# Crossbar-DMA transposes and full-array scores in a fused recurrent-attention and feed-forward kernel

## The chip, the cores and the metric

The kernel runs on one core of one Trainium2 chip. The time is device microseconds of one execution of the whole program. Before the change it is 191.06 us, the median of 3 runs (190.56, 191.06, 191.49). Beside the runs there is one profiled execution, from which all views of the profile come.

The core has a matrix engine (TensorE, PE in the profile; its weight loads are PEld), a vector engine (DVE), an activation engine (ACT), GpSimd (POOL) and SyncE (SP). SP computes nothing here: it issues every DMA of this kernel, in program order, on one queue.

## What is computed

Gated linear attention with a decay per key channel, then a feed-forward layer with a squared relu:

```python
# q, k, v, alpha: (4, 8, 768, 48), alpha in 0.8 to 1.0; w_in: (384, 2048); w_out: (2048, 384)
for t in range(S):
    state = alpha[:, :, t, :, None] * state + einsum('bhd,bhe->bhde', k[:, :, t], v[:, :, t])
    y[:, :, t] = einsum('bhd,bhde->bhe', q[:, :, t], state)
x = y.transpose(0, 2, 1, 3).reshape(3072, 384)
h = maximum(x @ w_in, 0)
out = (h * h) @ w_out          # (3072, 384) float32
```

## The kernel before

**Tiling.** The 4 x 768 tokens are 24 chunks of 128 tokens (6 for each batch entry). A chunk of the attention part makes one token tile of x, and the feed-forward part (called MoE in the code) works on tiles of 128 tokens, in groups of 4, 1, 1, and then 2.

**A chunk of attention** (`add_chunk(s)`, from line 358). Four loads of 192 KB bring alpha, q, k and v. ACT takes the logarithm of alpha (L379); a matmul with a triangular matrix sums it along the tokens (p0); ACT makes A, the exponential of the sum, and its inverse (L408, L412). DVE makes qA = q times A (L431) and kI = k times the inverse (L434), in bf16, with each head padded from 48 to 64 columns, so that two heads fill 128 columns. POOL casts v to bf16 (vb, L388). Then:

- p1q and p1k (L438 to L447): four PE transposes of 128x128 each, of qA and of kI, into one PSUM bank pT.
- cp, cpk (L449 to L458): copies from PSUM to the SBUF tile qkT, whose first four blocks are q transposed and whose last four are k transposed. Chunks 0 to 3 (`EARLY`) make two copies of 128x512, the others one of 128x1024 on DVE.
- p2 (L460 to L467): the scores sc, eight matmuls with 64 rows each: head `2p` lies in partitions 0 to 63 and head `2p+1` in 64 to 127 of block p.
- sm (L472): two masked products on DVE from PSUM to SBUF.
- ps, stm, sb (L482 to L498): the state, updated from kI and vb, decayed on DVE, cast on ACT for the next chunk.
- p3a, p3b: the output of the chunk, from q transposed and the state, and from sm and vb. xn (ACT), p4 (three PE transposes) and xT (DVE) put it into xT_big as the feed-forward's input.

kI, qA and the logarithm have 4 buffers each (`NBUF`), loads 6 (`LB`), qkT 4, r 8, the output tiles 6.

**The feed-forward part.** add_moe1: matmuls with w_in, a relu on ACT to r (L577), its square on DVE to gT (L585). add_moe2: 16 matmuls with w_out for a tile, a copy from PSUM (L617, or L615 on DVE), and an output DMA (L622).

**The order.** Nothing is scheduled at run time: each engine runs its instructions in the order in which they are written. That order comes from `Plan.run`, a list scheduler in the kernel's own Python, which works with planned durations. Each `Op` has an engine (or several to choose from), a duration, what it depends on, a priority, the PSUM bank it takes, and a latency `lat` after its end. The scheduler picks what can start earliest, then the lower priority number; attention has -10, MoE matmuls 0 or 0.1. `ready` adds a slack for PE to every dependency on another engine: 0.05, and 0.25 after the first 25 planned us. "DMA" is the planner's engine for loads, in their given order; "OUT" stands for output DMAs, which also take time from "DMA". `late` puts an operation further back in the final order than it was planned. At the end all operations are sorted by their planned start and written out, so the loads and outputs of SP's queue stand in that order too.

**The gate.** A chunk's p0 may be planned only when its number is at most `LEAD` (3.5) plus the tiles of MoE work already planned; each tile counts 2.56 for w_in and 2.56 for w_out.

Of the kernel before, what the change touches and what calls it, by code (L numbers as in the profile page):

```python
# [9 lines left out]
BF16 = mybir.dt.bfloat16  # L10
# [23 lines left out]
LAT = {"PE": 0.13, "ACT": 0.14, "DVE": 0.13, "POOL": 0.25}  # L34
PE_SLACK = 0.05
PE_CALM = 25.0


class Op:
# [15 lines left out]
def after(op, x=0.0):  # L55
    return (op, x)


class Plan:
# [13 lines left out]
    def ready(self, op):  # L73
        t = op.at
        slack = PE_SLACK if "PE" in op.durs else 0.0
        if slack and self.free.get("PE", 0.0) > PE_CALM:
            slack = 0.25
        for d, x in op.deps:
            if d.done is None:
                return None  # L80
            if x is None:
                t = max(t, d.done + (slack if d.eng != "PE" else 0.0))
            else:
                t = max(t, d.start + d.dur + x)
        if op.takes is not None:
            best = None
            for sl in op.takes:
                f = sl.free_at()
                if f is not None and (best is None or f < best):
                    best, op.slot = f, sl  # L90
            if best is None:
                return None
            t = max(t, best)
        return t

    def run(self, gate):
        free = self.free
        while any(self.pending.values()):
            best = None
            for eng, ops in self.pending.items():  # L100
                t0 = free.get(eng, 0.0)
                pick = None
                fifo = eng in ("DMA",)
                for op in (ops[:1] if fifo else ops):
                    if not gate(op):
                        continue
                    r = self.ready(op)
                    if r is None:
                        continue
                    if len(op.durs) > 1:  # L110
                        ends = {e: max(r, free.get(e, 0.0)) + x + LAT[e] for e, x in op.durs.items()}
                        if ends[eng] > min(ends.values()):
                            continue
                    key = (max(r, t0), op.prio)
                    if pick is None or key < pick[0]:
                        pick = (key, op)
                if pick is not None and (best is None or pick[0][0] < best[0]):
                    best = (pick[0][0], eng, pick[1])
            assert best is not None, "nothing can run"
            t, eng, op = best  # L120
            for e in op.durs:
                self.pending[e].remove(op)
            op.eng, op.dur = eng, op.durs[eng]
            op.start = t + getattr(op, "late", 0.0)
            free[eng] = t + op.dur
            if op.lat is None:
                op.lat = LAT.get(eng, 0.2)
            if eng == "OUT":
                free["DMA"] = max(free.get("DMA", 0.0), t) + op.dur
            op.done = t + op.dur + op.lat  # L130
            if op.takes is not None:
                self.ready(op)
                op.slot.release.append(op.gives if op.gives is not None else op)
            self.order.append(op)
            self.on_pick(op)
        self.order.sort(key=lambda o: o.start)
# [3 lines left out]
def kernel(  # L140
# [10 lines left out]
    nc = tc.nc  # L151
    B, H, S, D = q.shape
    HD = H * D
    P = 128
    DP = 64
    NP = H // 2
# [14 lines left out]
    big = ctx.enter_context(tc.tile_pool(name="big", bufs=1))  # L171
    LB = 6
    loads = ctx.enter_context(tc.tile_pool(name="loads", bufs=LB))
    work = ctx.enter_context(tc.tile_pool(name="work", bufs=4))
# [17 lines left out]
        out=utri_f, in_=utri_f, compare_op=ALU.is_ge, fill=0.0,  # L192
# [10 lines left out]
    for c in range(JN):  # L203
        blk = slice(JP * c, JP * c + JP)
        nc.gpsimd.affine_select(
            out=tri4[blk, 0:JW], in_=tri4[blk, 0:JW], compare_op=ALU.is_ge, fill=0.0,
# [17 lines left out]
    nc.gpsimd.memset(qA_s[:, :, :, D:], 0.0)  # L224
    kI_s = big.tile([P, NBUF, H, DP], BF16)
    nc.gpsimd.memset(kI_s[:, :, :, D:], 0.0)
    ae_s = big.tile([P, NBUF, NP, 2], FP32)
    nc.vector.memset(ae_s, 0.0)
    xT_big = big.tile([P, KT, n_tok], BF16)
# [4 lines left out]
    def pin(ins):  # L234
        tc.keep_in_program_order(ins)

    def mm(*a, **kw):
        pin(nc.tensor.matmul(*a, **kw))  # L238

    def tr(*a):  # L240
        pin(nc.tensor.transpose(*a))  # L241

    plan = Plan()
    sl_sc = Slots(1)
# [3 lines left out]
    GLA_BANKS = sl_bank[0:2]  # L248
# [12 lines left out]
    def add(eng, dur, emit, *deps, **kw):  # L261
        return plan.add(Op(eng, dur, emit, deps, **kw))
# [41 lines left out]
    C = [dict() for _ in range(NT)]  # L304
    state = {}
    SRC = dict(srcs)
    EARLY = 4

    JLD = 1.18
    J = {}  # L310
# [47 lines left out]
    def add_chunk(s):  # L358
        d = C[s]
        b, c = divmod(s, NCH)  # L360
        i = s % NBUF
        L, qA, kI, ae = L_s[:, i], qA_s[:, i], kI_s[:, i], ae_s[:, i]
        old = C[s - NBUF].get("end") if s >= NBUF else None
        g = dict(prio=-10.0 + s * 0.01)
        last = c == NCH - 1

        def cast(op, out_t, in_t):
            if op.eng == "ACT":
                pin(nc.scalar.copy(out_t, in_t))  # L369
            elif op.eng == "DVE":  # L370
                pin(nc.vector.tensor_copy(out_t, in_t))  # L371
            else:
                pin(nc.gpsimd.tensor_copy(out_t, in_t))
# [8 lines left out]
        else:  # L382
            ln = [add("ACT", 0.41, e_ln, d["ld_at"], old, prio=-15.0 if s < EARLY else -5.0)]
            d["use_at"] = ln[0]
# [50 lines left out]
        mq = d["use_qt"] = add("DVE", 0.47, e_qA, a_, d["ld_qt"], old, **g)  # L435
        mk = d["use_kt"] = add("DVE", 0.47, e_kI, ai, d["ld_kt"], old, **g)
# [6 lines left out]
        def e_p1k():  # L443
            for p in range(NP):
                tr(d["pT"][:, NP + p, :], kI[:, 2 * p:2 * p + 2, :], ident_bf)
        p1q = plan.add(Op("PE", 0.22, e_p1q, [mq], takes=GLA_BANKS, **g))
        p1k = plan.add(Op("PE", 0.22, e_p1k, [mk, after(p1q)], lat=0.15, **g))  # L447

        def e_cp(lo, hi):  # L449
            if lo == 0:  # L450
                d["qkT"] = work.tile([P, 2 * NP, P], BF16, name="qkT")
            cast(cpk if lo else cp, d["qkT"][:, lo:hi, :], d["pT"][:, lo:hi, :])
        if s < EARLY:
            cp = add({"ACT": 0.49, "DVE": 0.34}, 0, lambda: e_cp(0, NP), p1q, **g)
            cpk = add({"DVE": 0.34, "ACT": 0.49}, 0, lambda: e_cp(NP, 2 * NP), p1k, after(cp, -9.0), **g)
        else:
            cp = cpk = add("DVE", 0.61, lambda: e_cp(0, 2 * NP), p1k, **g)
        p1q.gives = cpk  # L458

        def e_p2():  # L460
            sc = d["sc"] = ps_sc.tile([P, 2, NP, P], FP32, name="sc")
            t = d["qkT"]
            for p in range(NP):
                for hh in range(2):
                    sl = slice(64 * hh, 64 * hh + 64)
                    mm(sc[:, hh, p, :], lhsT=t[sl, NP + p, :], rhs=t[sl, p, :], start=True, stop=True)
        p2 = plan.add(Op("PE", 0.42, e_p2, [cp, cpk], takes=[sl_sc], lat=0.10, **g))  # L467

        def e_sm(hh):
            if hh == 0:  # L470
# [60 lines left out]
        def e_xT():  # L531
            cast(xT, xT_big[:, :, s * P:(s + 1) * P], d["px"])
        xT = add({"ACT": 0.36, "DVE": 0.27} if s < EARLY else "DVE", 0.27, e_xT, p4, prio=-9.0)
        d["x"] = d["end"] = xT
# [95 lines left out]
    for d in DMA_ORDER + list(range(6, NT)):  # L630
        if d in ("i", "o"):
            load_w(d)
        elif d == "at":
            add_joint_alpha()
        elif isinstance(d, tuple):
            add_load(*d)
            if d == JLAST:
                for s in range(JN):
                    add_chunk(s)
        else:  # L640
            for nm, _ in srcs:
                add_load(d, nm)
            add_chunk(d)
# [23 lines left out]
                b2 = add_moe2(g, tt, b2, {}, range(NQ), M2_LAST if g >= NG - 2 else M2_BANKS)  # L667
        sq[(g, "free")] = b2

    LEAD = 3.5  # L670

    def gate(op):
        s = getattr(op, "gla", None)
        if s is not None:
            return s <= LEAD + (prog["m1"] + prog["m2"]) / 5.12
        return True
# [58 lines left out]
```

## Time and profile before

| what | value |
|---|---|
| runs | 191.06 us median of 3, 190.56 to 191.49 |
| span of the profiled execution | 189.9 us |
| copies to qkT of 128x1024, DVE, x20 | 690 ns each |
| copies to qkT of 128x512, DVE x3, ACT x5 | 422 and 588 ns each |
| qA, kI on DVE, x24 each | 572 and 576 ns each |
| masked scores sm on DVE, x48 | 683 ns each |
| square gT on DVE, x96 | 428 ns each |
| relu r on ACT, x96 | 604 ns each |
| first matmul (p0) of chunks 5, 11, 12, 13, 16, 22, 23 | 43.9, 76.5, 83.4, 90.3, 111.7, 154.0, 161.2 us |
| last load issued; last chunk's xT | 122.0; 169.7 us |

Times inside the program count from the start of the span. In a row of a timeline the first number is the start and the second how long it lasted; for rows with xN, N instructions are merged. A matmul's end is modelled, so neighbouring rows overlap and it is the starts that tell the pace. In a row of the windows the busy time of each engine in that stretch stands with its count of instructions. In the rows of DMA issues the last number is the median time in us from issue to landing.

### The profile page before, as it was taken

The page shows a single profiled execution, that of the slowest core. Times are in us where ns is not written, and L with a number is a line of the kernel's source. Part 1 is how long each engine was busy: PE and PEld are TensorE (multiplying, and loading weights), DVE is VectorE, ACT ScalarE, POOL GpSimd, SP SyncE. Part 2 cuts the span into 40 slices and gives each one's busy share as a digit, 9 for nine tenths or more (in the row PEclk, how much of TensorE's full clock was granted, in tenths as well). Part 3 has the DMA queues.
Part 4 walks back from the last instruction along what each step waited for, and adds up shares of the span by engine and source line. Part 5 has one row for each costly group of instructions (what it writes and reads, how often), then busy time and mean ns, then how long its engine had stood idle before and what let it go on. Part 6 is the DMA issues. An engine that isn't in the chain of part 4 may idle for free.

```text
span 189.9 us, 5238 instructions
## 1 busy us (share of the span) xinstructions
PE 181.7 (96%) x2092; PEld 137.6 (72%) x2092; DVE 127.5 (67%) x277; ACT 123.6 (65%) x285; POOL 17.5 (9%) x43
## 2 busy tenths in 40 slices
PE   7898999589999999999999999999999999999993
PEld 2577899357886788868868868868868768768661
DVE  1388889554798999858768768767857857734200
ACT  4667789155897778956955955946956746718321
POOL 8130100101111111121010010010010000000000
PEclk9999999999999999999999999999999999999999
DMA  6999996989999898999999899550110110111012
GB/s 181 226 242 264 299 342 133 350 227 196 246 234 223 183 219 188 213 175 226 202 209 232 174 239 214 108 149 0 43 45 0 47 41 5 41 41 45 12 71 83
DMA packets 104728, 30.22 MB, mean 159 GB/s; under 512 B 96256, under 2 KB 103936, under 8 KB 104704
## 3 DMA queue, kind: packets, MB, share of 16 engines
q1 hardware_dynamic: 104704, 29.89, 67.2%
q8 instruction: 16, 0.26, 0.6%
q14 instruction: 8, 0.07, 0.1%
HBM read 25.17 MB, written 4.72 MB: 157 GB/s over the span
## 4 chain that ended last, share of the span: by engine, by line
PE 84%; DMA 9%; ACT 2%; DVE 2%; issue 1%
PE bank L238 71%; DMA wo<-in_moe_w_out_dram 9%; PE bank L241 8%; PE sc L238 4%; PE st L238 2%; ACT w_out_b L294 1%; DVE w_out_b L292 1%; DVE qkT L371 0%; ACT qkT L369 0%; DVE st L492 0%; ACT A L408 0%; ACT ob L617 0%; DVE w_in_b L292 0%; DVE gT L585 0%; ACT Ainv L412 0%
## 5 line engine op out<-in xcount | busy, mean ns | idle before, releaser
L238 PE MATMUL bank<-xT_big,w_in_b 128*128 128x256 bf16 (+1 forms) x720 | 76.8, 251 | 0.0
L238 PE MATMUL bank<-w_out_b,gT 128*128 128x384 bf16 x384 | 71.6, 326 | 2.1 <-DVE w_out_b L292 2.1
L577 ACT ACTIVATE r<-bank 128x512 bf16<-128x512 f32 x96 | 56.5, 604 | 16.9 <-PE bank L238 14.9
L238 PEld LDWEIGHTS <-w_in_b 128*128 128x128 bf16 x720 | 55.4, 98 | 5.0
L238 PEld LDWEIGHTS <-gT 128*128 128x128 bf16 x400 | 35.6, 97 | 21.0 <-issue 2.1
L585 DVE TENSOR_TENSOR gT<-r 128x512 bf16<-128x512 bf16 x96 | 38.6, 428 | 14.2 <-ACT r L577 13.9
L472 DVE TENSOR_TENSOR sm<-sc,utri_b 128x512 bf16<-128x512 f32 x48 | 30.8, 683 | 3.2 <-PE sc L238 3.0
L617 ACT COPY ob<-bank 128x384 f32<-128x384 f32 x23 | 11.0, 478 | 23.7 <-PE bank L238 23.7
L431 DVE TENSOR_TENSOR qA_s<-qt,A 128x384 bf16<-128x384 f32 x24 | 13.7, 572 | 17.4 <-ACT A L408 17.4
L388 POOL CAST vb<-vt 128x384 bf16<-128x384 f32 x24 | 12.9, 538 | 122.1 <-DMA vt<-in_v_dram 64.0
L371 DVE COPY qkT<-bank 128x1024 bf16<-128x1024 bf16 (+1 forms) x23 | 15.0, 655 | 6.8 <-PE bank L241 6.8
L238 PEld LDWEIGHTS <-qkT 64*128 64x128 bf16 (+1 forms) x272 | 10.9, 95 | 6.7 <-issue 1.9
L408 ACT ACTIVATE A<-bank 128x384 bf16<-128x384 f32 x24 | 12.0, 498 | 4.9 <-PE bank L238 4.7
L497 ACT CAST sb<-st 128x384 bf16<-128x384 f32 x20 | 9.6, 478 | 7.9 <-DVE st L492 7.6
L434 DVE TENSOR_TENSOR kI_s<-kt,Ainv 128x384 bf16<-128x384 f32 x24 | 13.8, 576 | 0.0
L369 ACT CAST xn<-bank 128x384 bf16<-128x384 f32 x24 | 11.6, 483 | 1.5 <-PE bank L238 1.5
L379 ACT ACTIVATE L_s<-at 128x384 bf16<-128x384 f32 x20 | 10.5, 524 | 2.8 <-DMA at<-in_alpha_dram 2.6
L412 ACT ACTIVATE Ainv<-bank 128x384 bf16<-128x384 f32 x24 | 12.0, 502 | 0.0
L238 PE MATMUL bank<-warm 128*128 128x256 bf16 (+1 forms) x48 | 10.0, 345 | 1.3 <-DVE warm L186 1.2
L492 DVE TENSOR_TENSOR st<-st,ae_s 128x384 f32<-128x384 f32 x20 | 11.1, 556 | 0.0
L371 DVE COPY xT_big<-bank 128x384 bf16<-128x384 bf16 x23 | 8.1, 350 | 2.6 <-PE bank L241 2.5
L241 PE MATMUL bank<-ident_bf,kI_s 128*128 128x128 bf16 x96 | 9.3, 219 | 0.5 <-ACT qkT L369 0.5
(52 smaller groups left out, 138.0 us busy)
## 6 DMA issues: line engine op xcount, KB each, us to landing
qt<-in_q_dram SPq DMA_DIRECT2D x24, 192.0 KB, 3.8
kt<-in_k_dram SPq DMA_DIRECT2D x24, 192.0 KB, 3.8
vt<-in_v_dram SPq DMA_DIRECT2D x24, 192.0 KB, 3.9
out_dram<-ob SPq DMA_DIRECT2D x24, 192.0 KB, 2.7
at<-in_alpha_dram SPq DMA_DIRECT2D x20, 192.0 KB, 3.9
wo<-in_moe_w_out_dram SPq DMA_DIRECT2D x4, 768.0 KB, 9.0
wi<-in_moe_w_in_dram SPq DMA_DIRECT2D x4, 384.0 KB, 5.0
wi<-in_moe_w_in_dram SPq DMA_DIRECT2D x2, 768.0 KB, 8.3
```

What stands on the lines that cost most here:

```text
L238: pin(nc.tensor.matmul(*a, **kw))
L241: pin(nc.tensor.transpose(*a))
L369: pin(nc.scalar.copy(out_t, in_t))
L371: pin(nc.vector.tensor_copy(out_t, in_t))
L388: pin(nc.gpsimd.tensor_copy(d["vb"], d["vt"]))
L408: pin(nc.scalar.activation(d["A"], d["pm"][:, 0:HD].rearrange("p (h d) -> p h d", h=H), AF.Exp))
L412: pin(nc.scalar.activation(d["Ai"], d["pm"][:, 0:HD].rearrange("p (h d) -> p h d", h=H), AF.Exp, scale=-1.0))
L431: pin(nc.vector.tensor_mul(qA[:, :, 0:D], d["qt"], d["A"]))
L434: pin(nc.vector.tensor_mul(kI[:, :, 0:D], d["kt"], d["Ai"]))
L472: pin(nc.vector.tensor_mul(d["sm"][:, hh], d["sc"][:, hh], utri_b.to_broadcast([P, NP, P])))
L577: pin(nc.scalar.activation(box["r"][:, 0:w], box["ph"][:, 0:w], AF.Relu))
L585: pin(nc.vector.tensor_mul(gT[g][:, f0:f0 + per, lo * P:lo * P + n], r, r))
```

## The change

From chunk 11 on (`TURN`), q and k are transposed by two DMA transposes on SP's queue (`dma_start_transpose`, SBUF to SBUF, 128 x 512 bf16 each) straight into qkT; the eight PE transposes and their PSUM bank fall away. The planner knows them as a new engine "TR", with 0.6 us each, a latency of 6.0 and `late` 0.3; like outputs they also take planned time from "DMA".

From chunk 4 on the scores use the whole array: k transposed is copied into kz, a tile of zeros in which each head has its own 128-row block, so that the other head's 64 rows are zero, and the matmul takes all 128 rows of q. kz has two buffers and is cleared once on POOL. In chunks 4 to 10 the two kz copies read PSUM (DVE or ACT, as the planner finds), and qkT gets q alone, copied by DVE; in chunks 11 to 23 they read qkT in SBUF, on DVE.

The plan changes as well: the slack of attention's PE operations after 25 planned us is 0.25, then 0.4 from 48 and 1.2 from 85; p2 is planned at 0.45 (full) or 0.53 in place of 0.42; `LEAD` becomes 5.0.

```diff
+GLA_SLACK = [(0.0, 0.25), (48.0, 0.4), (85.0, 1.2)]
...
             slack = 0.25
+            if op.prio < -1.0:
+                slack = [x for at, x in GLA_SLACK if self.free["PE"] > at][-1]
...
-            if eng == "OUT":
+            if eng in ("OUT", "TR"):
                 free["DMA"] = max(free.get("DMA", 0.0), t) + op.dur
...
+    NKZ = 2
+    kz_s = big.tile([P, NKZ, NP, 2, P], BF16)
+    nc.gpsimd.memset(kz_s, 0.0)
...
+    TURN, TLD, TLAT, TLATE = 11, 0.6, 6.0, 0.3
...
+        def e_turn(src, lo):
+            if lo == 0:
+                d["qkT"] = work.tile([P, 2 * NP, P], BF16, name="qkT")
+            pin(nc.sync.dma_start_transpose(out=d["qkT"][:, lo:lo + NP, :], in_=src.rearrange("p h d -> p (h d)")))
+        turned = s >= TURN
+        if not turned:
+            p1q = plan.add(Op("PE", 0.22, e_p1q, [mq], takes=GLA_BANKS, **g))
+            p1k = plan.add(Op("PE", 0.22, e_p1k, [mk, after(p1q)], lat=0.15, **g))
...
-        if s < EARLY:
+        def e_kz(hh):
+            rows = slice(DP * hh, DP * hh + DP)
+            src = d["qkT"] if turned else d["pT"]
+            cast(ks[hh], kz_s[rows, s % NKZ, :, hh, :], src[rows, NP:2 * NP, :])
+        full = s >= EARLY
+        if turned:
+            cp = add("TR", TLD, lambda: e_turn(qA, 0), mq, lat=TLAT)
+            cpk = add("TR", TLD, lambda: e_turn(kI, NP), mk, after(cp, -9.0), lat=TLAT)
+            cp.late = cpk.late = TLATE
+            ks = [add("DVE", 0.21, lambda hh=hh: e_kz(hh), cpk, C[s - NKZ]["p2"], **g) for hh in range(2)]
+        elif full:
+            cp = add("DVE", 0.34, lambda: e_cp(0, NP), p1k, **g)
+            ks = [add({"ACT": 0.49, "DVE": 0.34}, 0, lambda hh=hh: e_kz(hh), p1k, C[s - NKZ]["p2"], **g)
+                  for hh in range(2)]
+            p1q.gives = cp
+        else:
             cp = add({"ACT": 0.49, "DVE": 0.34}, 0, lambda: e_cp(0, NP), p1q, **g)
             cpk = add({"DVE": 0.34, "ACT": 0.49}, 0, lambda: e_cp(NP, 2 * NP), p1k, after(cp, -9.0), **g)
-        else:
-            cp = cpk = add("DVE", 0.61, lambda: e_cp(0, 2 * NP), p1k, **g)
-        p1q.gives = cpk
+            ks = [cpk]
+            p1q.gives = cpk
...
+                    if full:
+                        mm(sc[:, hh, p, :], lhsT=kz_s[:, s % NKZ, p, hh, :], rhs=t[:, p, :], start=True, stop=True)
+                        continue
...
-        p2 = plan.add(Op("PE", 0.42, e_p2, [cp, cpk], takes=[sl_sc], lat=0.10, **g))
+        p2 = d["p2"] = plan.add(Op("PE", 0.45 if full else 0.53, e_p2, [cp, *ks], takes=[sl_sc], lat=0.10, **g))
...
-    LEAD = 3.5
+    LEAD = 5.0
```

More of the change, by code (lines that the diff above doesn't have):

```diff
@@ L445, in e_p1k @@
                 tr(d["pT"][:, NP + p, :], kI[:, 2 * p:2 * p + 2, :], ident_bf)
-        p1q = plan.add(Op("PE", 0.22, e_p1q, [mq], takes=GLA_BANKS, **g))
-        p1k = plan.add(Op("PE", 0.22, e_p1k, [mk, after(p1q)], lat=0.15, **g))
+        def e_turn(src, lo):
[6 more added lines that the diff above has]
+            p1k = plan.add(Op("PE", 0.22, e_p1k, [mk, after(p1q)], lat=0.15, **g))
         def e_cp(lo, hi):
```

## The prediction, made before the changed kernel was run

> **What bounds the kernel now.** I read the page first. TensorE (PE) is busy for 96% of the span and the chain that ended last is 84% PE, with 9% for one stretch of DMA:
>
> ```profile
> PE 181.7 (96%) x2092; PEld 137.6 (72%) x2092; DVE 127.5 (67%) x277; ACT 123.6 (65%) x285; POOL 17.5 (9%) x43
> ...
> DMA  6999996989999898999999899550110110111012
> ...
> PE 84%; DMA 9%; ACT 2%; DVE 2%; issue 1%
> ...
> qt<-in_q_dram SPq DMA_DIRECT2D x24, 192.0 KB, 3.8
> ...
> out_dram<-ob SPq DMA_DIRECT2D x24, 192.0 KB, 2.7
> ...
> wo<-in_moe_w_out_dram SPq DMA_DIRECT2D x4, 768.0 KB, 9.0
> ```
>
> The reader is to see that the DMA engines are full to about slice 25 of 40 (some 120 us) and nearly empty after it, and how long a transfer takes from issue to landing: 2.7 us for an output, 3.8 behind other loads, 9.0 for a large weight piece.
>
> A busy PE need not be a full one, because its ends are modelled. So I read the PE timeline by starts, in the steady part (here the chunk whose transposes stand at 128 us):
>
> ```profile
> 128.15 0.39 PE L241 MATMUL bank<-ident_bf,qA_s 128*128 128x128 bf16 x4
> 128.37 0.39 PE L241 MATMUL bank<-ident_bf,kI_s 128*128 128x128 bf16 x4
> 128.59 0.33 PE L238 MATMUL st<-vb,kI_s 128*128 128x96 bf16 x4
> 128.76 1.15 PE L238 MATMUL bank<-xT_big,w_in_b 128*128 128x256 bf16 x9
> 129.84 0.40 PE L238 MATMUL sc<-qkT 64*128 64x128 bf16 x8
> 130.17 1.16 PE L238 MATMUL bank<-xT_big,w_in_b 128*128 128x256 bf16 x9
> ```
>
> Each group starts where the one before has streamed out: 4 transposes take 0.22 us (0.055 each), and elsewhere 15 matmuls of 256 columns take 1.63 (133.46 to 135.09; 0.109 each). From 42 us to the last matmul there is hardly a hole of another kind. So what leaves PE there leaves the time. Before 42 us PE waits for weights: the chain has 9.63 and 8.38 us of DMA for w_out pieces, and PE stands for 2.1 us until the second is cast. The change moves no load ahead of that point, so I let these 42 us stand.
>
> Then the other engines, by windows (length, PE, PEld, DVE, ACT, POOL busy, clock, DMA share, GB/s):
>
> ```profile
> 48.00:55.00 7.00, 7.00 (x125) 6.05 (x120) 6.45 (x14) 6.04 (x16) 0.60 (x2) 1.00 1.03 242
> ...
> 69.00:76.00 7.00, 7.00 (x96) 6.12 (x97) 7.00 (x17) 5.98 (x16) 0.51 (x1) 1.00 0.95 199
> ...
> 83.00:90.00 7.00, 7.00 (x88) 5.34 (x86) 5.00 (x11) 4.88 (x12) 1.03 (x2) 1.00 0.99 207
> ...
> 132.00:139.00 7.00, 7.00 (x83) 5.53 (x80) 5.77 (x14) 5.50 (x14) 0.51 (x1) 1.00 0.09 32
> ```
>
> From 83 us on DVE and ACT have a fifth or more of their time free; at 69 to 76 DVE has none. The granted clock is 1.00 throughout.
>
> **Transposes removed (chunks 11 to 23).** 8 PE transposes go from each of 13 chunks. By the rows above 8 take 0.44 us: 13 x 0.44 = **-5.7 us** of PE. Their weight loads run beside matmuls and count nothing.
>
> **Full-array scores (chunks 4 to 23).** The 64-row group stands between starts 128.76 and 130.17: 1.41 us, less nine matmuls of 0.109 (0.98), is 0.43 us. So 0.33 is its own and 0.10 is lost ahead of it. A full-array matmul of 128 columns has the transposes' 0.055: 8 x 0.055 = 0.44, up to 0.45. That is +0.01 to +0.02 for each of 20 chunks: **+0.3 us**. Were the 64-row pairs as cheap as four matmuls, 0.22, giving them up would cost 0.22 x 20 = 4.4 us, 4.1 more than I take. The Trainium skill, "TensorEngine Tiling (Array Packing)", section "Theoretical Speedup", says so, up to 2x for a contract dimension of 64 or less, and speaks against this part. The trace's 0.43 denies that here; the same page's "Key Properties" has a change of the tiling mode drain the array, which fits the 0.10 lost on entry.
>
> **Copies, chunks 4 to 10.** One DVE copy of 128x1024 (0.69) becomes one of 128x512 (0.42 on DVE by its three rows) and two of 64 rows x 512 from PSUM, as long as the 128-row ones (0.42 on DVE, 0.59 on ACT). With one on each engine DVE gains 0.42 + 0.42 - 0.69 = 0.15 and ACT 0.59 a chunk. Between 48 and 76 us DVE is busy 26.1 of 28 us and ACT 22.3; five chunks copy there, so +0.75 and +2.95: 26.9 and 25.2. It fits, barely. Besides, the plan frees pT's bank after the first copy, while the last of the three ends 0.17 (one on ACT) to 0.85 us (all on DVE) later; the next attention matmul that takes this bank, one of two, may wait so long. Bounds on PE: nothing, to 7 x 0.43, 3 us. I take 0.3, as PE has no such hole now.
>
> **Copies, chunks 11 to 23.** 0.69 goes and two copies from SBUF come. No row shows such a one; the nearest are the square of 128x512 within SBUF, 0.43, and the memset of as many bytes (L186), 0.27. DVE changes by -0.15 to +0.17 a chunk beside its fifth free: no price.
>
> **The DMA transposes.** Two of 128 KB a chunk on SP's queue, each behind a wait for DVE (qA, then kI). No crossbar transpose is in the trace. Time in the queue: loads of 192 KB leave SP's queue four to 4.35 us with some outputs between (at-issues at 59.79 and 116.34 are 13 chunks apart), about 1 us each; 128/192 of that is 0.65; the bounds are 0.4 (by bytes at the 350 GB/s of the best slice) and 1.0 (a load whole). I take 0.65, nearest by size. Landing: from 2.7 us (the output, queue empty) to 9.9 (the longest load, which sat behind a w_out piece). I take 4 to 5: a load's 3.8 (from 50 us on 5.6 at most) and a little for the second of the pair. The plan places the scores 0.6 + 6.0 after the transfer's start, then two DVE copies, then a slack of 1.2; PE waits only if the landing takes over **7.8 us**. So I cost it at nothing; what hides it is 6 us more latency per chunk covered by MoE matmuls, which the lead supplies.
>
> Queued behind a transpose that waits on SP are the loads and outputs. Loads are early: the vb casts, which follow their load at once, run for chunk 13 at 81.1 us and chunk 16 at 94.6, while the chunks' first matmuls come at 90.3 and 111.7. Outputs hold only an opool buffer of six. 7 chunks x 2 x 0.65 = 9 us more for a queue full until 122.8 us still ends near 132, and the last chunk begins at 161.
>
> **Lead and slack.** Counting MoE matmuls ahead of each chunk's first matmul, attention runs 1.6 to 3.25 tiles ahead for chunks 5 to 9 (the loads hold it) and exactly 3.50 from chunk 10 on (the gate holds it). So 5.0 acts from chunk 10, where it pulls some 1.5 chunks forward, about 4 us of DVE work each (two products 0.57, two masked scores 0.68, state 0.56, two copies), to a place where DVE is full. What hides it is the eight r buffers: squares may lag by 8 x 0.43 = 3.4 us. Price 0 to 3 us; I take 0.3. More slack moves attention matmuls back, and MoE matmuls fill; it can gain at most the rest of the holes after 42 us, under 1 us. I take none.
>
> **Smaller.** The memset of kz is 2048 columns: 4 x 0.52 = 2.1 us on POOL ahead of the memset that ends at 5.51. It then ends at 7.6; the first reader of those pads is the totals' matmul at 11.9, and the first vb cast is at 9.8. Nothing.
>
> **Sum.** -5.7 + 0.3 + 0.3 + 0.3 = -4.8. The profiled execution has a span of 189.9; the runs' median of 191.06 is 1.2 above it, which I take to lie around the span and to stay: 191.06 - 4.8 = **186.3 us**.
>
> **Rivals.**
> *Late landings (slower).* If a transpose lands d us after the 7.8 that the plan covers, PE stands at the scores. Everything shifts, and as the next chunk's transposes were already issued, the delay grows by d about every second chunk: 6.5 d over 13 chunks. It eats the gain at d = 0.75, a landing of 8.5 us; at 9.9 it is 6.5 x 2.1 = 13.7, so 200. For: queues full until 120 us, 9.0 us for the w_out pieces. Against: from 50 us on no load takes over 5.6 us to land and no output over 5.1, and after 123 us the queue is nearly empty. Chance 0.15.
> *Transposes one block at a time.* Eight blocks a chunk; if each paid the 2.7 us of an output alone, 21.6 us a chunk against a period of 7.1: 13 x 21.6 from 78 us is 359, plus 20 for what follows, some 380. For: nothing here. Chance 0.03. The Trainium skill, "VectorE: DVE Perf Modes", section "The three transpose paths", has a rule of this kind: TensorE 390 ns for a 128x128 block, the crossbar 1309, so TensorE where PSUM will do. As an estimate by that page, 8 x 1.309 = 10.5 us a chunk would give about 78 + 136 + 20 = 234.
> *DVE and ACT crowd PE at 48 to 83 us.* Their bounds in place of my 0.6 share one overload: to +3, so 188.7. For: DVE 7.00 of 7.00. Against: PE had no hole there even so. Chance 0.12.
> *The ring falls behind.* At 1.0 us each instead of the planned 0.6, 7 chunks x 2 x 0.4 = 5.6 us late while loads last; 7.8 - 3.8 = 4.0 is covered, 1.6 is paid: 187.9; at 1.3 each it is 9.8 - 4 = 5.8 and all is gone. Chance 0.08.
> *PE's freed time stays empty* because MoE's own ACT and DVE set the pace: 191. Against: 5.5 and 5.8 of 7. Chance 0.02. *Scores that cost 4.1 us more* by the doubling above: 186.3 + 4.1 = 190.4, against the 0.43 measured. Chance 0.01.
>
> **Numbers.** Forecast, 185.3 to 187.5: 0.59. The range also takes in the crowded and the ring case and the bounds of the unknown prices, 184.8 (no price for crowding, some holes gained) to 191.5; left out are late landings and serial blocks, about 0.18. Runs of this kernel spread by some 0.5%, so that is the bound of no change (190.1 to 192.0). Faster: 0.59 + 0.12 + 0.07 of the ring, less 0.02 for crowding beyond its bound: 0.76. Same: that 0.02, 0.01 of the ring, 0.02 of empty time, 0.01 of costly scores and 0.01 of the landings: 0.07. Slower: 0.14 + 0.03 = 0.17.
>
> **What would show it.** PE's count falls by 104 transposes. The scores start 0.109 after a 256-column matmul, with 0.44 to the next. The period of chunks in the steady part falls from 7.1 to about 6.7. Landing of the transposes under 7.8 us and no PE wait on a DMA or on kz proves the cover; waits at the scores from chunk 11 on prove the first rival, holes at 48 to 83 us the third. Wrong it would be if the landing were over 8.5 us.

## The result, and the profile after

The changed kernel takes **197.78 us** (median of four runs, 196.23 to 198.54) against 191.07 for the kernel before on the same chip: 1.0364 times as long, with a 95% interval of 1.0316 to 1.0412. It is 6.7 us slower by the medians and 6.9 by the ratio, where I had forecast 4.8 us faster. Each ratio here and below compares the fast runs of a kernel with the fast runs of the kernel before on the same chip, so it can differ a little from the quotient of two medians. The profiled execution took 198.54 us, the longest of the four, and has a span of 196.8, against 189.9 before.

The page of the changed kernel, busy time first, then the granted clock and the DMA share in 40 slices, then the shares of the chain that ended last:

```profile
PE 180.6 (92%) x1982; PEld 138.1 (70%) x1982; DVE 128.4 (65%) x298; ACT 126.5 (64%) x291; POOL 19.6 (10%) x44
...
PEclk9999999999999999999999999958999999999999
DMA  6999997989999991788999879899999124110022
...
PE 51%; DMA 20%; DVE 10%; ACT 10%; SPq 4%; issue 3%; POOL 1%; ACTq 0%; POOLq 0%; DVEq 0%
```

PE has 110 matmul records fewer than before, 104 of them the transposes. Yet its busy share fell from 96% to 92% in a longer span, and the chain, which had been 84% PE, is now 51% PE and 20% DMA. The clock has a dip to half in one place. The DMA row is full to about slice 30 (148 us), where it was to slice 25 (120 us), with a gap at slice 15 (74 to 79 us).

Where PE stands shows in the windows (length; busy time and count of PE, PEld, DVE, ACT, POOL; clock, DMA share, GB/s). Those shown of before had 7.00 us of PE and a clock of 1.00 in each:

```profile
48.00:55.00 7.00, 6.68 (x115) 6.22 (x116) 6.16 (x15) 5.35 (x14) 0.76 (x2) 1.00 1.05 245
55.00:62.00 7.00, 6.70 (x87) 4.98 (x85) 5.87 (x15) 5.60 (x16) 0.77 (x2) 1.00 1.05 219
62.00:69.00 7.00, 6.37 (x87) 5.09 (x86) 5.21 (x12) 5.36 (x16) 1.06 (x2) 1.00 0.99 220
69.00:76.00 7.00, 5.86 (x78) 4.95 (x76) 5.92 (x14) 6.15 (x16) 0.51 (x1) 1.00 0.89 172
76.00:83.00 7.00, 6.70 (x80) 6.09 (x80) 6.94 (x18) 6.37 (x17) 0.51 (x1) 1.00 0.39 80
...
125.00:132.00 7.00, 3.94 (x33) 2.89 (x31) 3.92 (x10) 2.82 (x6) 0.51 (x1) 0.69 0.97 213
132.00:139.00 7.00, 7.00 (x61) 5.00 (x59) 3.70 (x10) 3.92 (x10) 1.29 (x2) 0.82 0.98 194
```

There are two kinds of loss. From 48 to 83 us PE misses 2.7 us in small pieces. From 125 to 132 it misses 3.06 in one piece, and then runs at a lower clock. The timelines of PE and of ACT there (start, duration, engine, line, what; in brackets the idle time ahead and who ended it):

```profile
125.23 0.33 PE L244 MATMUL st<-vb,kI_s 128*128 128x96 bf16 x4
128.62 0.80 PE L244 MATMUL bank<-xT_big,w_in_b 128*128 128x256 bf16 x3 [3.06 <-ACT r L607]
129.22 0.53 PE L244 MATMUL bank<-sb,qkT 128*128 128x96 bf16 x4
129.54 2.12 PE L244 MATMUL bank<-xT_big,w_in_b 128*128 128x256 bf16 x9
131.46 0.53 PE L244 MATMUL bank<-L_s,utri_b 128*128 128x384 bf16 x1
```

```profile
123.76 0.17 ACT L425 ACTIVATE ae_s<-bank 64x4 f32<-64x4 f32 x1
127.43 0.52 ACT L386 ACTIVATE L_s<-at 128x384 bf16<-128x384 f32 x1 [3.50 <-DMA at<-in_alpha_dram]
127.98 1.09 ACT L607 ACTIVATE r<-bank 128x512 bf16<-128x512 f32 x2
```

Read the second block first. ACT stands for 3.50 us at the logarithm of a later chunk's alpha (L386), which has not been loaded. The relus (L607) behind it have their input, but ACT runs in order. PE's next matmul needs a PSUM bank that such a relu empties, so PE stands until the first relu has run (3.06 us). Then nine matmuls of 256 columns take from 129.54 to 131.46, 0.213 each instead of 0.109. In windows of half a us the granted clock falls at about 127.7, while PE still stands, is 0.50 from 128.0 on, and is back at about 134.5:

```profile
127.50:128.00 0.50, 0.00 (x0) 0.00 (x0) 0.14 (x1) 0.47 (x2) 0.00 (x0) 0.68 1.14 223
...
134.50:135.00 0.50, 0.50 (x6) 0.32 (x4) 0.34 (x1) 0.10 (x1) 0.00 (x0) 0.99 0.97 197
```

From the first matmul at 128.62 on that is 5.9 us of work at half rate, so some 3 us are lost to it: as much as to the hole itself. This is the profiled run. Its mean granted clock is 0.98; the other three have 0.991, which leaves room for about half of such a loss (0.009 of 195 us is 1.8 us, 0.02 of 196.8 is 3.9), and they took 196.23 to 198.38 us. So the clock's part differs from run to run.

This alpha was issued late. SP's queue, at the first transposes and near the hole:

```profile
71.47 1.00 SPq L361 DMA_DIRECT2D vt<-in_v_dram  x1
77.77 1.29 SPq L456 DMA_TRANSPOSE qkT<-qA_s  x1
79.11 0.56 SPq L361 DMA_DIRECT2D at<-in_alpha_dram  x1
79.77 1.21 SPq L456 DMA_TRANSPOSE qkT<-kI_s  x1
...
121.38 1.75 SPq L361 DMA_DIRECT2D kt<-in_k_dram  x1
123.23 0.53 SPq L361 DMA_DIRECT2D vt<-in_v_dram  x1
123.80 0.60 SPq L361 DMA_DIRECT2D at<-in_alpha_dram  x1
```

SP issues nothing from 72.47 to 77.77: it stands at the first transpose, which waits for qA (5.2 us), and loads stand behind it. That is slice 15 of the DMA row, and the 80 GB/s of the window 76 to 83. The next load in the queue, the alpha of chunk 13, could have gone: its buffer had been free since the logarithm of chunk 7, which starts at 53.26. The alpha issued at 123.80 is the one whose logarithm starts at 127.43. The waits in total (us, times, longest) name the same things:

```profile
ACT L_s L386 <- DMA at<-in_alpha_dram: 11.2, 7, 3.5
...
DVE kz_s L378 <- ACT kz_s L376: 4.2, 6, 0.7
...
PE bank L244 <- ACT r L607: 3.1, 1, 3.1
...
ACT kz_s L376 <- DVE qkT L378: 2.2, 4, 1.1
```

Before, the logarithm waited 2.6 us for alpha in all. The transposes themselves, by the DMA rows (count, median us from issue to landing), land soon:

```profile
q1 hardware_dynamic: 118848, 33.30, 75.7%
...
qkT<-qA_s SPq DMA_TRANSPOSE x13, 3.2
qkT<-kI_s SPq DMA_TRANSPOSE x13, 3.2
```

The queue's share gives their price on the DMA engines: 75.7% of 196.8 us less the 67.2% of 189.9 before is 21.4 us, over 26 transposes 0.82 us of all 16 engines each.

### The profile page after: what moved, and what is told of

The parts are those of the page before. It is cut to its first block, busy times and chain, and to the rows that moved or that the text cites. A ratio compares the mean times of both kernels' runs of the same rounds, so it can differ in the third digit from the quotient of the medians.

```text
span 196.8 us, 5076 instructions
## 1 busy us (share of the span) xinstructions
PE 180.6 (92%) x1982; PEld 138.1 (70%) x1982; DVE 128.4 (65%) x298; ACT 126.5 (64%) x291; POOL 19.6 (10%) x44
## 3 DMA queue, kind: packets, MB, share of 16 engines
q1 hardware_dynamic: 118848, 33.30, 75.7%
## 4 chain that ended last, share of the span: by engine, by line
PE 51%; DMA 20%; DVE 10%; ACT 10%; SPq 4%; issue 3%; POOL 1%; ACTq 0%; POOLq 0%; DVEq 0%
PE bank L244 44%; DMA at<-in_alpha_dram 8%; DMA wo<-in_moe_w_out_dram 8%; DMA vt<-in_v_dram 4%; ACT r L607 4%; PE sc L244 3%; SPq L361 3%; DVE sm L502 3%; PE bank L247 3%; DVE kz_s L378 1%; ACT kz_s L376 1%; DVE st L522 1%; DVE gT L615 1%; SPq L456 1%; ACT L_s L386 1%
## 5 line engine op out<-in xcount | busy, mean ns | idle before, releaser
L244 PE MATMUL bank<-xT_big,w_in_b 128*128 128x256 bf16 (+1 forms) x720 | 79.0, 255 | 3.7 <-ACT r L607 3.1
L607 ACT ACTIVATE r<-bank 128x512 bf16<-128x512 f32 x96 | 56.9, 608 | 15.4 <-PE bank L244 13.8
L244 PEld LDWEIGHTS <-w_in_b 128*128 128x128 bf16 x720 | 57.4, 99 | 10.6 <-issue 4.2
L395 POOL CAST vb<-vt 128x384 bf16<-128x384 f32 x24 | 13.2, 552 | 131.1 <-DMA vt<-in_v_dram 104.9
L647 ACT COPY ob<-bank 128x384 f32<-128x384 f32 x20 | 9.6, 481 | 14.8 <-PE bank L244 14.7
L386 ACT ACTIVATE L_s<-at 128x384 bf16<-128x384 f32 x20 | 10.4, 521 | 11.3 <-DMA at<-in_alpha_dram 11.2
L244 PE MATMUL sc<-qkT,kz_s 128*128 128x128 bf16 x160 | 12.9, 220 | 1.2 <-DVE kz_s L378 0.9
L522 DVE TENSOR_TENSOR st<-st,ae_s 128x384 f32<-128x384 f32 x20 | 11.2, 560 | 3.5 <-PE st L244 1.2
L441 DVE TENSOR_TENSOR kI_s<-kt,Ainv 128x384 bf16<-128x384 f32 x24 | 13.2, 551 | 0.1
L244 PEld LDWEIGHTS <-kz_s 128*128 128x128 bf16 x160 | 10.1, 98 | 3.7 <-DVE kz_s L378 2.8
L244 PE MATMUL bank<-warm 128*128 128x256 bf16 (+1 forms) x42 | 8.5, 337 | 1.3 <-DVE warm L189 1.3
L244 PE MATMUL bank<-vb,sm 128*128 128x48 bf16 x192 | 9.2, 185 | 0.3 <-DVE sm L502 0.3
L244 PEld LDWEIGHTS <-sm 128*128 128x128 bf16 x192 | 8.2, 97 | 1.8 <-DVE sm L502 0.6
```

Of the source, the lines that this page charges most:

```text
L386: pin(nc.scalar.activation(L[:, :, 0:D], d["at"], AF.Ln))
L395: pin(nc.gpsimd.tensor_copy(d["vb"], d["vt"]))
L441: pin(nc.vector.tensor_mul(kI[:, :, 0:D], d["kt"], d["Ai"]))
L522: pin(nc.vector.tensor_mul(st4, st4, bcast(ae, D)))
L607: pin(nc.scalar.activation(box["r"][:, 0:w], box["ph"][:, 0:w], AF.Relu))
```

## The experiments

Three parts of the change can be at fault: the copies of the early chunks (theory: they crowd or hold PSUM), the transposes (their landing, or what they do to the loads), and the plan's slack and lead alone. "After" below is the changed kernel, "before" the one before; each ratio is to before, with its interval.

**One part undone at a time.** `e1` and `e4` move the first chunk with DMA transposes, to never and to 18. What isn't transposed by DMA then uses the padded copies from PSUM, up to chunk 23 and 17.

```diff
-    TURN, TLD, TLAT, TLATE = 11, 0.6, 6.0, 0.3
+    TURN, TLD, TLAT, TLATE = 99, 0.6, 6.0, 0.3    # e1; 18 in e4
```

> The changed kernel with TURN = 99: all chunks keep their PE transposes; full-array scores, slack and lead 5.0 stay. Theory S (starved loads: the DMA transposes hold SP's queue, the alpha loads come late, ACT's logarithm waits for them in order and the relus behind it hold PE's banks): loads go at about 4.4 us a chunk again, ACT's waits on alpha fall from 11.2 to under 3 us, the 3 us hole and the low clock after it are gone; 191.1 + 0.3 for the scores + up to 2.7 for the holes at 48 to 83 us = 191.5 to 194. Theory C (crowding: the early copies and the longer lead are the cause, whoever transposes): holes stay and 5.7 us of PE work come back: 199 or more.

> The changed kernel with TURN = 18: DMA transposes only for the six chunks that come about when the loads are over. Theory S: loads at their old pace, no late alpha, 6 x 0.44 = 2.6 us of transposes off PE: 191.1 + 0.3 + up to 2.7 - 2.6 = 189 to 192. Theory C: the copies and the lead are unchanged, so 196 to 199.

Measured: 200.7 us, 1.0434 [1.0369, 1.0499], and 195.91, 1.0194 [1.0117, 1.0271]. So the transposes do gain (six chunks of them 4.8 us, partly because PSUM copies go with them), and there is a slowdown without any (though `e1` has the copies from PSUM in 13 chunks more). In neither does the logarithm wait for alpha as it does after (1.1 us in both).

`e2` takes the lead back, with everything else as after:

```diff
-    LEAD = 5.0
+    LEAD = 3.5
```

> The changed kernel with LEAD = 3.5 as before, DMA transposes kept. Theory S: the loads stay at about 6.5 us a chunk, but chunks need them 1.5 tiles later, so the alpha waits shrink to a few us and the hole at 125 us is gone: 187 to 192. Theory C: the holes at 62 to 76 us shrink, those after 110 stay: 194 to 196. Against both: with less lead the transposes' latency shows at the scores and it is slower than 198.

Measured: 204.65, 1.0614 [1.051, 1.0718], the slowest of all. The transposes land about as they did after (medians 3.4 and 2.5 us), and the alpha waits fall to 1.2, but the kz copies now wait 7.9 us for the transpose in four places, up to 3.9 each. Without the lead the latency shows; the lead hides most of it (after has one such wait, 0.9 us).

`e3` keeps the transposes and the plan, and gives chunks 4 to 10 their old copy of 128x1024 and 64-row scores:

```diff
-        full = s >= EARLY
+        full = turned
...
+            p1q.gives = cp
+        elif s >= EARLY:
+            cp = add("DVE", 0.61, lambda: e_cp(0, 2 * NP), p1k, **g)
+            ks = [cp]
```

> The changed kernel with chunks 4 to 10 as before (one copy of 128x1024, 64-row scores); chunks 11 to 23 as changed. Theory S: only the 2.7 us of holes at 48 to 83 us can go, the late hole stays: 194 to 197. Theory C: most of the loss goes: 190 or less.

Measured: 195.41, 1.0184 [1.0097, 1.0271]. The early padded copies cost 1.8%, 3.4 us (uncertain by some 2); the rest stays. Its hole lies elsewhere, of the same kind: 2.72 us at 113.80, with the logarithm waiting 10.5 us for alpha in all.

**The plan alone.** `e6` is `e3` with no DMA transposes at all (`TURN = 99`), so before with slack, lead and p2's planned time of the change; `e9` and `e10` put the lead and the slack into before, one at a time.

```diff
...
-    LEAD = 3.5
+    LEAD = 5.0          # e9
...
+            if op.prio < -1.0:          # e10, with GLA_SLACK of the change
+                slack = [x for at, x in GLA_SLACK if self.free["PE"] > at][-1]
```

> Slack, lead 5.0 and the planned 0.53 of the scores alone: no DMA transpose, no zero-padded keys (64-row scores and one copy from chunk 4 on). If the copies for the padded keys made the holes of e1: 190.5 to 192.5. If slack and lead made them: 196 to 200, as in e1 less 0.3.

> The kernel before with LEAD = 5.0 and nothing else. The plan alone cost 1.2% (e6). If pulling 1.5 chunks forward into the stretch where DVE is full is the cause: holes at 62 to 83 us as in e6, 192 to 194, and the steady part after 97 us as before. If the longer lead is hidden: 190 to 191.5.

> The kernel before with the new slack of attention's PE operations and nothing else (lead 3.5). If the slack is the cause of e6: 192 to 194, with later attention starving the MoE matmuls or lost overlap. If only the lead is: 189.5 to 191.5.

Measured: 193.85, 1.0122 [1.003, 1.0213]; 193.67, 1.0058 [1.0015, 1.0101]; 192.03, 1.0039 [1.0002, 1.0075]. The plan costs about 1.2%, 2.3 us, to which lead and slack give 0.6% and 0.4% by themselves. In the profile of `e6` (the longest of its four runs, span 193.3) PE has these holes where chunks are pulled forward:

```profile
62.00:69.00 7.00, 5.73 (x89) 4.18 (x87) 6.01 (x12) 4.18 (x12) 1.17 (x2) 1.00 0.91 195
69.00:76.00 7.00, 7.00 (x97) 6.07 (x95) 6.98 (x15) 6.50 (x19) 0.59 (x2) 1.00 0.94 199
76.00:83.00 7.00, 6.57 (x89) 5.44 (x87) 7.00 (x16) 5.67 (x14) 1.28 (x2) 1.00 1.09 216
...
97.00:125.00 28.00, 28.00 (x309) 21.09 (x308) 19.70 (x42) 18.57 (x47) 2.88 (x5) 1.00 0.89 188
```

```profile
67.73 0.33 PE L244 MATMUL bank<-sb,qkT 128*128 128x96 bf16 x4 [1.22 <-DVE qkT L378]
```

PE misses 1.70 us from 62 to 83. Most of it is one wait of 1.22 us for a copy that DVE makes behind two masked products; the stretch in which DVE is full comes after it (69 to 83) and costs 0.43. From 97 on PE misses nothing. Another 1.25 us of this profile are lost before 40 us: the first matmul with w_out starts at 39.35, against 38.10 before.

**Turned chunks only where loads are nearly over.** `e7` is `e3` with `TURN = 18`; `e8` is `e7` with 64-row scores throughout (`full = False`, `ks = [cpk]`), so no padding anywhere.

> DMA transposes and padded keys for chunks 18 to 23 alone, chunks 4 to 17 as before, slack and lead of the change. If copies from PSUM and starved loads are the two causes, both are gone and 6 x 0.44 = 2.6 us are won: 187.5 to 190. If slack and lead cost time: 193 or more.

> As e7, but the scores of chunks 18 to 23 use 64 rows straight from the transposed keys, with no padded copies. The scores cost PE 0.43 in place of 0.45 and DVE loses two copies of 0.29 a chunk; if padding is of no use on PE: equal to e7 within 0.5%. If 64-row groups cost more than the 0.10 on entry: slower than e7.

Measured: 191.06, 1.0013 [0.9971, 1.0055], and 190.8, 0.9997 [0.9954, 1.0039]. Against `e6`, six chunks of DMA transposes bring 1.1%, 2.1 us (uncertain by about as much, as `e6` has an interval of 0.9% each way), where 6 x 0.44 = 2.6 were to go from PE. Padding makes no difference in these chunks.

**The transposes as load on the queue.** `e5` leaves before's transposes on PE and adds the 26 DMA transposes, into a tile that nobody reads:

```diff
...
+        if s >= 11:
+            t0 = add("TR", 0.6, lambda: e_turn(qA, 0), mq, lat=6.0)
+            t1 = add("TR", 0.6, lambda: e_turn(kI, NP), mk, after(t0, -9.0), lat=6.0)
+            t0.late = t1.late = 0.3
```

`e13` is `e5` with them issued by ACT (`nc.scalar`) instead of SP.

> The kernel before with 26 DMA transposes added (chunks 11 to 23, at the places and with the planned costs of the change) into a spare tile that nobody reads; PE transposes, 64-row scores and lead 3.5 stay, and the transposes are extra work beside the reference's. Theory S: loads slow from 4.4 to over 6 us a chunk; with the lead of 3.5 attention needs them later, so either the alpha waits come back and it takes 193 to 198, or the six load buffers cover it and it takes 191 to 193. If transposes cost the queue nothing: 190.5 to 192 with loads at their old pace.

> As e5 (26 transposes into a spare tile nobody reads, beside the unchanged work), but issued from ACT's queue, so that SP issues loads and outputs alone. If the transposes' time on the DMA engines slows the loads: alpha loads still about 6.3 us a chunk between 72 and 110 us. If SP's issue does: 4.4 us a chunk as before. Either way ACT loses 2 x 1.2 us of issue a chunk, so the time should be 193 to 200.

Measured: 192.69, 1.007 [1.0019, 1.012], and 200.53, 1.0479 [1.0417, 1.0541]. The price on the DMA engines can be read again, in `e13` on a queue of its own (packets, MB, share):

```profile
q10 hardware_dynamic: 14144, 3.41, 10.3%
...
spare<-qA_s ACTq DMA_TRANSPOSE x13, 4.5
spare<-kI_s ACTq DMA_TRANSPOSE x13, 4.0
```

10.3% of 199.0 us over 26 is 0.79 us; `e5` gives 0.82. The pace of the loads, from one alpha issue to the next, was 4.35 us a chunk before. It is 6.54 after (79.11 to 144.46, ten chunks), 6.34 in `e5` (72.51 to 135.93, ten) and 5.5 in `e13` (78.94 to 117.30, seven). Count the transposes issued in these stretches: 10 in `e13`, 16 in `e5`, 19 after. In `e13` 7 x 4.35 + 10 x 0.79 = 38.4 us is all of the 38.36 measured, so there the loads are slower by the time of the transfers alone, as far as this sum goes. On SP's queue the sum leaves 6.8 us (`e5`: 43.5 + 13.1 of 63.42) and 6.3 us (after: 43.5 + 15.6 of 65.35), some 0.6 to 0.7 a chunk. That goes with the transposes' place in this queue, but what in it costs the time wasn't taken apart. `e13` shows too that an issue isn't free for the engine that makes it: 26 x 1.2 us went into ACT's stream. And `e5` slows the loads as much as after, but costs 0.7%: with before's lead the logarithm waits 6.2 us for alpha, none longer than 2.2. It takes both, slower loads and attention that runs 1.5 tiles further ahead.

`e11` takes after and puts the transposes 2 planned us further back in SP's order, so that more loads pass them:

```diff
-    TURN, TLD, TLAT, TLATE = 11, 0.6, 6.0, 0.3
+    TURN, TLD, TLAT, TLATE = 11, 0.6, 6.0, 2.3
```

> The changed kernel with the DMA transposes 2.0 us further back in SP's order (TLATE 2.3 in place of 0.3), so that qA and kI are ready when SP comes to them. If SP's waiting in front of a transpose is what starves the loads: its waits on that line fall from 36 to under 10 us, the alpha waits from 11 to under 6, and it takes 192.5 to 195.5; landings stay under the covered 7.8 us, so no new wait at the scores. If it is the time that transposes take in the queue: the loads stay at about 6.5 us a chunk and it takes 196 to 199.

Measured: 197.43, 1.0276 [1.0216, 1.0336]. It regains 0.9%, no more; the pace is 6.49 (76.24 to 141.14, ten chunks) and alpha is still waited for 10.6 us. The edit didn't do what it was for: SP's waits ahead of the transposes add up to 33.8 us, against 35.6 after. So it doesn't tell whether SP's standing still or the transposes' time in the queue slows the loads.

**The test of the cause.** `e14` is after with one edit: from chunk 12 on alpha, and alpha alone, is loaded through ACT's queue, past everything on SP's.

```diff
-            pin(nc.sync.dma_start(out=d[nm], in_=SRC[nm][b, c]))
+            eng = nc.scalar if nm == "at" and s >= 12 else nc.sync
+            pin(eng.dma_start(out=d[nm], in_=SRC[nm][b, c]))
```

> The changed kernel with the alpha loads of chunks 12 to 23 issued from ACT's queue; all else as changed. If alpha's place behind transposes and other loads in SP's order makes ACT wait: the alpha waits go from 11 to under 3 us, the hole and the low clock at 125 us go, and of the 6 us lost there most comes back: 191 to 195. If the DMA engines' time is what is short: q, k and v stay late, DVE waits in ACT's place, and it takes 195 to 198.

Measured: 191.76, **0.9986 [0.9949, 1.0024]**; 3.8% of before's time is back, a little more than the whole loss of 3.6%, by an edit that takes no byte off the DMA engines. Its waits and windows:

```profile
POOL vb L396 <- DMA vt<-in_v_dram: 99.1, 18, 13.4
...
ACT L_s L387 <- DMA at<-in_alpha_dram: 1.2, 1, 1.2
```

```profile
97.00:125.00 28.00, 28.00 (x319) 22.83 (x317) 22.97 (x56) 20.66 (x51) 2.54 (x5) 1.00 1.14 205
125.00:140.00 15.00, 14.91 (x152) 11.70 (x149) 11.88 (x28) 11.08 (x28) 1.76 (x3) 1.00 1.11 204
```

The v loads still come late (the casts wait 99.1 us; after 104.9, before 64.0), the alpha waits have fallen from 11.2 to 1.2, and the hole and the dip of the clock have gone. In after the two windows have 26.90 of 28 and 11.94 of 15, at 1.00 and 0.77. It was alpha's place in the queue, not the loads' bandwidth: the DMA engines carry more here (shares of 1.14 and 1.11, after 0.93 in the first of these windows and 0.97 in the second). The edit also takes twelve issues off SP's queue, and from 85 us on its v loads are issued every 5.7 us, where after it was 6.2; what that gives by itself wasn't tried. Up to 76 us `e14` keeps the holes of after (6.77, 6.70, 6.37, 5.57 in the first four windows).

**A better version.** The rest follows from the parts: old copies and 64-row scores, and lead and slack only as far as the transposes need them.

```diff
-GLA_SLACK = [(0.0, 0.25), (48.0, 0.4), (85.0, 1.2)]
+GLA_SLACK = [(0.0, 0.25), (72.0, 1.2)]
...
-            return s <= LEAD + (prog["m1"] + prog["m2"]) / 5.12
+            return s <= min(LEAD, 3.5 + 0.3 * max(0, s - 8)) + (prog["m1"] + prog["m2"]) / 5.12
```

This is `e17`: `e8` with that, p2 planned at 0.42, `TURN = 12` and alpha on ACT's queue. `e12` and `e15` are on the way to it, with `TURN` 18 and 15 (ramp from chunk 14 and 11, slack from 112 and 92) and alpha on SP; `e16` is `e15` with alpha on ACT.

> DMA transposes for chunks 18 to 23 alone, no padded keys, old early copies, the slack of 1.2 only from 112 planned us on, and a lead that rises from 3.5 at chunk 14 to 5.0 at chunk 19. If the three causes found so far (early copies, starved loads, lead into a full DVE) are all: 190.6 - 2.6 = 188 (187 to 189.3). If the transposes cost what they save: 190 to 191.5.

> As e12, with DMA transposes from chunk 15 on, the lead rising from chunk 12 and the slack of 1.2 from 92 planned us. If the loads are so far ahead that six more transposes do not starve them: 3 x 0.44 = 1.3 us under e12, 187.5 to 189. If they do: equal to e12 or slower, with alpha waits over 3 us.

> As e15 with the alpha loads of chunks 12 to 23 issued from ACT's queue. In e15 ACT waits only 0.3 us on alpha, so if late alpha is the only harm that transposes in the load stage do: equal to e15 within 0.5%. If loads were late there in another way: up to 1% faster.

> As e16 with DMA transposes from chunk 12 on, the lead rising from chunk 9 and the slack of 1.2 from 72 planned us. If alpha past the queue is all that early transposes need: 3 x 0.44 = 1.3 us under e16, 187 to 188.5. If the earlier lead meets the full DVE again, as in e9: equal to e16 or up to 1% slower, with holes at 62 to 97 us.

Measured: 189.8, 0.9881 [0.983, 0.9932]; 189.71, 0.9871 [0.9823, 0.992]; 188.59, 0.9898 [0.9846, 0.995]; and **186.67, 0.9794 [0.9756, 0.9832]** for `e17`, faster than both kernels. The ramp, with p2's planned time and the slack that goes with it, is worth 1.2% over `e8`. From 15 turned no gain of alpha on ACT can be told; from 12 it wasn't tried without. One hole is left in `e17`, 1.21 us at 73.15, where PE waits for DVE's kI of the last chunk that PE transposes:

```profile
62.00:69.00 7.00, 7.00 (x97) 5.71 (x95) 6.74 (x16) 6.10 (x17) 0.61 (x2) 1.00 1.11 230
69.00:76.00 7.00, 5.79 (x82) 4.80 (x82) 6.18 (x13) 5.57 (x15) 1.26 (x2) 1.00 1.12 234
76.00:83.00 7.00, 7.00 (x82) 5.85 (x82) 6.68 (x16) 6.73 (x18) 0.51 (x1) 1.00 0.57 111
...
97.00:125.00 28.00, 27.98 (x305) 20.79 (x303) 19.73 (x43) 19.23 (x47) 2.58 (x5) 1.00 1.06 211
```

## Why the prediction was wrong, and where it was right

**The sum of the runs.** Plan alone (`e6`) +1.2%, transposes on top (`e3`) +0.6%, early copies on top (after) +1.8%: 2.3 + 1.2 + 3.4 = 6.9 us. The second term hides two: the transposed chunks saved PE some 5.4 us as worked out, and paid it and 1.2 more for late alphas. `e14` removes the lateness and moves 7.2 us, and 1.2 - 7.2 = -6.0 is near the -5.7 + 0.3 of the forecast. Each of these differences is uncertain by 1 to 2 us, so the sum is an account that fits and no proof of each term; the 0.6% alone can't be told from nothing.

**The step that failed** is "Queued behind a transpose that waits on SP are the loads and outputs. Loads are early", costed at nothing. I had the right queue and the wrong consumer. I compared v's cast with the chunk's first matmul, nine to seventeen us apart, and the end of the loads with the last chunk. The consumer that matters is ACT's logarithm of alpha, which stands ahead of the first matmul in an engine that runs in order, with the relus of the feed-forward part behind it. The trace of before had it already, for chunks 14 and 15:

```profile
81.56 0.52 ACT L379 ACTIVATE L_s<-at 128x384 bf16<-128x384 f32 x1 [0.72 <-DMA at<-in_alpha_dram]
86.10 0.52 ACT L379 ACTIVATE L_s<-at 128x384 bf16<-128x384 f32 x1 [1.03 <-DMA at<-in_alpha_dram]
```

The first matmuls of these chunks come at 97.39 and 104.64, some 16 and 18 us later, and yet ACT waits for alpha: the loads had no time to spare where they are used first. The prediction named nobody queued behind that wait. Its "9 us more for a queue full until 122.8 us still ends near 132" was low as well: the last load is issued at 147.38. The transfer time of a transpose was near (0.82 where I took 0.65, within 0.4 to 1.0), but the term was its time in the queue, and that was above the bound: the ten chunks of loads took 65.35 us in place of 43.5 with 19 transposes among them, 1.15 each. What I left out is SP standing still, 5.3 us at the first one, while loads with free buffers stand behind. The rival of the falling ring had the late transposes as its victim; it was the loads.

**Two terms were mis-sized.** The copies of chunks 4 to 10: taken at 0.3, with a bound of 3; measured 3.4 (the holes that wait for kz from 48 to 83 us add up to 2.5). The mechanism was the one I named. On DVE and ACT at 63 us of after:

```profile
63.78 0.42 DVE L378 COPY qkT<-bank 128x512 bf16<-128x512 bf16 x1 [0.81 <-PE bank L247]
64.30 0.58 ACT L376 COPY kz_s<-bank 64x512 bf16<-64x512 bf16 x1 [0.59 <-DVE qkT L378]
64.91 0.43 DVE L378 COPY kz_s<-bank 64x512 bf16<-64x512 bf16 x1 [0.70 <-ACT kz_s L376]
```

The three don't run side by side: each starts as the one before ends, though on two engines. They take 1.56 us in place of 0.69. My "0.17 to 0.85 us" after the first copy is 1.14, because ACT's copy doesn't overlap DVE's. The plan has given the bank away by then, and the matmul that takes it stands 0.63 us, until 65.39, for the last copy.

Lead and slack: taken at 0.3 and nothing, within 0 to 3; measured 2.3. I said that it pulls chunks "to a place where DVE is full" and trusted the r buffers to hide it. In `e6` PE does wait for DVE there (1.22 us), though for a copy of q and k and not for a square, so the r buffers were no cover for it; the windows in which DVE is full cost 0.43.

**What was right.** That eight transposes are 0.44 us of PE a chunk agrees with `e7` against `e6` (2.1 us for six chunks, against 2.6), within wide intervals. The scores on the whole array take 0.44 to 0.46 to the next start (after: 111.35 to 111.79; 60.09 to 60.55), without loss at their entry (21 matmuls of 0.109 from 109.06 end at 111.35), and padding is neither gain nor loss where it is fed from SBUF (`e8` against `e7`). The Trainium skill, "TensorEngine Tiling (Array Packing)", section "Theoretical Speedup", had it that half-height tiles could double the rate; no run here shows that. Landing was well under 7.8 us (median 3.2, 4.6 at most), and four blocks landed together, not one by one; so late landings, which I gave the most of my chances on the slower side, were not the cause. That with lead 3.5 the latency does show (`e2`) bears out that the lead supplies the cover. The clearing of kz cost nothing that shows (the first cast of v starts at 9.83, before at 9.82).

**What stays open.** It wasn't settled how much of the slower loads is SP standing still, since `e11` hardly changed that, and whether `e17` needs alpha on ACT's queue. The split of `e6`'s 1.2% rests on `e9` and `e10` alone, which add up to 1.0% with intervals nearly as wide, and 1.25 us of its profile are lost before 40 us, for which no cause was looked for.

## What to carry to other kernels

When an instruction that waits is put on a queue, look for the consumer of everything behind it on every engine that runs in order, and ask what stands behind *that* consumer; the earliest user of a late load isn't the one that its chunk's matmuls suggest. Time saved on the bounding engine arrives only if the loads can keep the pace that it then asks for: compute us per chunk for the queue (with its waits) and for the engine side by side. A planner's slack and lead should grow with what needs them, not be set for the whole run.

## What the runs showed of the hardware

- A crossbar transpose of 128 x 512 bf16 within SBUF holds the issuing queue for at least 1.19 us (medians 1.44 and 1.21 for qA and kI after, 1.21 on ACT in `e13`; the longest 2.67), takes 0.8 us of the 16 DMA engines, more than its share by bytes of a 192 KB load (0.65 of some 1 us), and landed 2.4 to 4.6 us after its issue (up to 6.7 in `e13`).
- A hole of 3.06 us on PE brought half the clock from about 127.7 us, 2.1 us after PE's last matmul had ended, to about 134.5: 6.8 us, 5.9 of them of work. In `e3`, after its hole of 2.72 us, the clock was at half from about 114.55 to 117.96, 3.4 us, and fell only 0.75 us after PE had started again. The Trainium skill, "TensorE: Matmul & The Clock Gate", section "Part 1: The HAM clock gate (the "warmup" mystery)", has a clock that halves after an idle window of about 3.4 us and comes back after about as long a busy one. The half rate agrees (0.213 against 0.109 us a matmul); both holes were shorter than that, and the way back took 5.9 us of work in one and 4.2 in the other (113.80 to 117.96).
- Copies by DVE and ACT from one PSUM bank into two tiles followed one another (0.42, 0.58, 0.43, each starting 0.1 or less after the other's end). The profile puts each wait down to the copy before it, by semaphore events, so here the program's own waits order them; whether they could overlap wasn't tried.
